# Window attention and a gated feed-forward on one core: neighbouring w_out rows, masks on TensorE, another order of loads

## Chip, core, metric

One core of one Trainium2 chip. The metric is the device time of one execution in microseconds; the number compared is the median of several executions. The engines are TensorE (PE, matmuls; its weight loads are PEld), VectorE (DVE), ScalarE (ACT), GpSimd (POOL) and SyncE (SP). Transfers are issued here from SyncE's queue and from GpSimd's, two from ScalarE's.

## What is computed

```python
# q, k, v: (4, 8, 768, 64) float32; n_sink = 4, window = 128
scores = (q @ k^T) / sqrt(64)
keep   = (key < 4) | ((0 <= query - key) & (query - key < 128))
a      = softmax(where(keep, scores, -1e9))
x      = (a @ v) with heads side by side          # (3072, 512)
h      = x @ w_in                                 # (3072, 2048)
g      = h * sigmoid(beta * h)                    # beta: one per column of h
out    = g @ w_out                                # (3072, 512) float32
```

The 2048 columns of h, the 2048 entries of beta and the 2048 rows of w_out belong together; any common order of them gives the same result.

## The kernel before

The 3072 tokens are eight blocks T of 384. A block's attention is four **units**, one for each pair of heads: units 0 to 3 make T=0, units 4 to 7 T=1, and so on to unit 31. Even blocks are the first half of a batch's sequence, odd ones the second half, whose queries also need the four sink keys.

A unit goes through these steps. q and k are loaded in float32 into a stage (`load_qk`, line 535, SyncE's queue), cast to bf16 on GpSimd or VectorE (`cast`, L650), transposed on TensorE into the PSUM bank "tr" (`transpose_in`, L663), and copied to SBUF (L670). TensorE makes the scores, ScalarE the exponential E, VectorE multiplies E by a 0/1 mask, TensorE multiplies E with v, the sink part first (L832), then the window (L843); a column of ones beside v gives the sums. VectorE takes their reciprocal (L852) and normalises (L854); the result is transposed (L871) and copied (L875) into xT, the input of the feed-forward. From unit 8 the last transpose, and from unit 12 the first one too, is done by the DMA; those later units have their q, k, v cast by the DMA on GpSimd's queue (`land_qk`, `land_v`).

Units 4 to 7 use `scores_by_banks`: the scores of a unit are split over two pairs of PSUM banks. Bank 0 has 512 columns for each head, bank 1 256 columns of window and 256 of sinks. Each bank has its own exponential (L795) and its own mask on VectorE (`mask_by_banks`, L804: 2x512 and 2x256 elements). Units 0 to 3 (`scores`, `PE_MASK` = 4) already mask on TensorE: a matmul of the identity with an additive mask (0 or -1e6) opens the accumulation, and the score matmuls add to it.

The feed-forward goes in **hidden blocks**: block i is the 128 columns m = i % 16 of h for the tokens of T = i // 16. Four matmuls of 384 columns (`hidden_matmul`, L887), a tanh on ScalarE (L895) and one operation on VectorE, the gate (L908), make g. Then **products** (`project`, L922) of 512 columns add g's part m times w_out's into an accumulator for each 128 tokens; after 16 of them the row block is copied and stored. Block T+1 of the hidden matmuls needs all four units of T+1.

w_in is loaded in four transfers, w_out in eight of two parts m each (`load_w_out`, L601, GpSimd's queue, cast to bf16 on the way). w_out's part m is the rows 128m to 128m+127, a row on each partition.

**The order on every engine is made by a planner** (class `Prog`): each operation has a guessed duration, and the planner simulates the engines and the queues and places at every step what can start first, the earlier in the program where two can. A DMA gets a landing time from sizes and rates (`transfer`), `TAIL` (900 ns) after its last byte, and some have an added lateness (`late`). The engines then execute that order strictly, waiting on semaphores wherever the guess was too early. Where the planner sees TensorE idle at the start, it inserts matmuls of ones (`filler`, L914), `MORE` (60 ns) beyond the hole it sees. The loads of SyncE's queue keep the program's order ("loads sp").

The part of the program that the change touches is written so:

```python
# steps s = -2 .. ; hidden block i = s for s < 16, then 8 steps without a block, then i = s - 8
casts = {-1: 4, 0: 5, 1: 6, 2: 7}          # casts of units 4 to 7
# units 4..7: transposes at s = 0..3, scores at s = 16..19, values at 17..20, out at 18..21
# products: none for s < 16, three a step in the 8 steps between, then two, then one a step
```

Of the kernel before, what the change touches and what calls it, by code (L numbers as in the profile page):

```python
# [11 lines left out]
DM, DF, NOUT = 512, 2048, 512  # L12
NTOK = B * S
# [5 lines left out]
TT = 384  # L19
# [27 lines left out]
PE_MASK = 4  # L47

# [49 lines left out]
class Prog:  # L98
# [14 lines left out]
    TAIL, MIX, HEAVY, RING = 900.0, 1.1, 2.5, 8  # L113
# [4 lines left out]
    IDLE, MORE, EARLY = 50.0, 60.0, 5500.0  # L118
# [251 lines left out]
def bass_streamingllm_window__then__act_swish_beta_kernel(  # L370
# [32 lines left out]
    beta_stage = sb("beta_stage", (16, 128), F32)  # L403
# [5 lines left out]
    ident32 = sb("ident32", (32, 32), F32)  # L409
    scratch = sb("scratch", (32, 1), F32)  # L410
    mask = [sb(f"mask{z}", (128, 6, 128), BF16) for z in range(2)]
    add_mask = sb("add_mask", (128, 6, 128), BF16)
    stage = {t: [sb(f"{t}_stage{z}", (128, 2, 6, D), F32) for z in range(4)] for t in "qk"}
# [116 lines left out]
    def load_qk(n, x, after=(), queue="sp"):  # L530
# [5 lines left out]
           dma=f"{name}{pb}_{half}", seq="loads " + queue, late=3300.0 if (n, x) == (4, 0) else 0.0,  # L536
# [55 lines left out]
    w_out_src = moe_w_out.rearrange("(m p) n -> p m n", p=128)  # L592
# [176 lines left out]
    def scores_by_banks(n):  # L769
# [3 lines left out]
        for bank, runs in enumerate(AT_ONCE[half]):  # L773
            of = 2 - 2 * bank
            names = HS_NAMES[of:of + 2]
            src = hs_ps[:, of:of + 2, :]
            with P.together("pe"):
# [7 lines left out]
                for kb, qb, nq in runs:  # L785
                    w = 128 * nq
                    for hh in range(2):
                        rows = slice(64 * hh, 64 * hh + 64)
                        op("pe", lambda e, at=at, w=w, kb=kb, qb=qb, nq=nq, hh=hh, rows=rows, of=of: e.matmul(  # L789
                            hs_ps[:, of + hh, at:at + w], keys_of(pb, rows, kb),  # L790
                            queries_of(pb, rows, qb, nq), start=True, stop=True),
# [7 lines left out]
    def mask_by_banks(n):  # L799
        z, half = n % NE, place(n)[2]  # L800
        for bank, cols in enumerate((slice(0, 512), slice(512, 768))):
            m = mask[half][:, :, :].rearrange("p m x -> p (m x)")[:, cols]
            w = cols.stop - cols.start
            op("dve", lambda e, m=m, cols=cols, w=w: e.tensor_tensor(  # L804
                E[z][:, :, cols], E[z][:, :, cols], m.unsqueeze(1).to_broadcast([128, 2, w]), ALU.mult),
               r=[("E", z, bank), *MASK[half]], w=[("E", z, bank)], **dve(580.0 if bank == 0 else 290.0))
# [77 lines left out]
    def hidden_matmul(i, c):  # L884
# [3 lines left out]
            bank, w_in16[:, c, m * 128:(m + 1) * 128], xT[:, c, T * TT:(T + 1) * TT],  # L888
# [31 lines left out]
    def project(T, t, m, bank, name, eng="act", cols=slice(0, NOUT), queue="sp"):  # L920
# [24 lines left out]
    op("act", lambda e: e.dma_start(beta_stage[:, :], moe_beta.rearrange("(m p) -> m p", p=128)),  # L945
       w=["beta_stage"], dma="beta", busy=500.0, lag=100.0)
# [6 lines left out]
    for c in range(3):  # L953
        load_v32(0, 1, c)
    op("act", lambda e: e.activation(scratch[:, :], ones32[:, 0:1], AF.Exp, bias=0.0, scale=1.0),
# [10 lines left out]
    select(ident32[:, :], ones32[:, :], [[1, 32]], ALU.is_equal, 0.0, 0, -1, ["ones32"], ["ident32"])  # L966
    transpose_first(0)
    op("pe", lambda e: nc.tensor.transpose(acc[1][:, 0:16], beta_stage[:, :], ident32[0:16, 0:16]),
       r=["beta_stage", "ident32"], w=["acc1"], **pe(64))
    op("dve", lambda e: e.tensor_scalar(beta_half[:, :], acc[1][:, 0:16], 0.5, None, ALU.mult),  # L970
       x=["acc1"], w=["beta"], **dve(100.0))
# [16 lines left out]
    for n in range(4):  # L988
# [4 lines left out]
        if n == 2:  # L993
# [4 lines left out]
            load_v32(1, 0, 0, [("w_in", 0, 4)])  # L998
            load_v32(1, 0, 1, [("w_in", 0, 4)])
            load_v32(1, 0, 2, [("w_in", 0, 4)])  # L1000
# [3 lines left out]
            load_qk(7, 1, [("w_in", 0, 4)])  # L1004
            load_v32(1, 1, 0, [("w_in", 0, 4)])
# [26 lines left out]
    for s in range(-2, S_END + NM):  # L1032
# [114 lines left out]
```

## Time and profile before

| | |
|---|---|
| three executions | 229.34, 230.49, 231.1 us; median 230.49 |
| the profiled execution | 229.0 us, of which the span of the instructions is 227.2 |
| granted TensorE clock | 1.00 throughout |
| busy: PE, DVE, ACT, POOL | 218.2, 133.0, 141.7, 125.4 us |
| weight loads PEld | 122.1 us, beside PE |
| moved by DMA | 29.7 MB in 98389 packets, 131 GB/s mean |
| first hidden block of T=0 / of T=1 | 17.07 us / 42.99 us from the span's start |

In a time order, a row gives start, length, engine, line, operation and tiles, how often, and in brackets how long the engine had been idle before and what ended that. The lengths shown for matmuls include their way through the array, so consecutive ones overlap; the distance between starts is what one costs in a run of them.

### The profile page before, as it was taken

To read this page: it belongs to the slowest core of one execution; us is meant where nothing else is said; L and a number is where in the kernel's file an instruction comes from. 1 tells how busy PE (TensorE), PEld (TensorE's weight loads), DVE (VectorE), ACT (ScalarE), POOL (GpSimd) and SP (SyncE) were. 2 spreads that over 40 slices of the span, in tenths; PEclk is the share of its full clock that TensorE was granted. 3 is DMA by queue.
4 is the path that set the end of the run, shared out by engine and by line. 5 is a ranking of instruction groups with operands and counts; after the bars stand their busy time and mean duration, and the time that the engine had idled before them with its cause. 6 is when DMAs were issued, how large, how long until landed. Compare 5 with 4: busy or idle time off the path is not lost.

```text
span 227.2 us, 4402 instructions
## 1 busy us (share of the span) xinstructions
PE 218.2 (96%) x1721; PEld 122.1 (54%) x1749; DVE 133.0 (59%) x263; ACT 141.7 (62%) x210; POOL 125.4 (55%) x193
## 2 busy tenths in 40 slices
PE   7999978899999999999999999999999999999995
PEld 4665545454655555555555555555555555555454
DVE  4756878459974666666565656555666564443200
ACT  3778796259855777666657676666656755555310
POOL 6692387999996969995939398876300000000000
PEclk9999999999999999999999999999999999999999
DMA  5999989999999989999979999999911112110122
GB/s 168 255 191 215 280 194 151 204 242 206 123 148 177 159 89 151 123 161 134 120 110 157 98 134 139 121 154 138 140 24 52 52 26 64 46 49 0 60 79 95
DMA packets 98389, 29.70 MB, mean 131 GB/s; under 512 B 84912, under 2 KB 95424, under 8 KB 98368
## 3 DMA queue, kind: packets, MB, share of 16 engines
q0 software_dynamic: 55888, 10.52, 58.2%
q1 hardware_dynamic: 42304, 18.75, 36.5%
q8 instruction: 14, 0.23, 0.4%
q10 hardware_dynamic: 176, 0.14, 0.2%
q14 instruction: 7, 0.06, 0.1%
HBM read 27.32 MB, written 6.29 MB: 148 GB/s over the span
## 4 chain that ended last, share of the span: by engine, by line
PE 73%; DMA 14%; SPq 6%; DVE 3%; issue 2%; POOL 1%; ACT 0%; ACTq 0%
PE hs_ps L887 31%; PE acc L922 30%; DMA k_stage<-in_k_dram 4%; PE hs_ps L754 4%; SPq L535 4%; PE hs_ps L843 3%; DMA q_stage<-in_q_dram 3%; DMA w_in<-in_moe_w_in_dram 3%; SPq L544 2%; DMA w_out<-in_moe_w_out_dram 2%; DMA xT<-o_norm 2%; PE hs_ps L922 2%; POOL qk L650 1%; PE hs_ps L832 1%; DVE g L908 1%
## 5 line engine op out<-in xcount | busy, mean ns | idle before, releaser
L895 ACT ACTIVATE th<-hs_ps,beta_half 128x384 f32<-128x384 f32 x120 | 69.3, 582 | 61.8 <-PE hs_ps L887 61.1
L887 PE MATMUL hs_ps<-xT,w_in 128*128 128x384 bf16 x480 | 96.2, 326 | 0.6 <-issue 0.2
L922 PE MATMUL acc<-w_out,g 128*128 128x512 bf16 x340 | 93.8, 380 | 1.3 <-issue 0.5
L908 DVE SCALAR_TENSOR_TENSOR g<-th,hs_ps 128x384 bf16<-128x384 f32 x120 | 65.5, 550 | 42.8 <-ACT th L895 41.3
L887 PEld LDWEIGHTS hs_ps<-xT,w_in 128*128 128x128 bf16 x480 | 45.6, 98 | 38.5 <-DVE g L908 1.2
L922 PEld LDWEIGHTS acc<-w_out,g 128*128 128x128 bf16 x368 | 33.6, 98 | 30.2 <-issue 3.8
L570 POOL DMA_DIRECT2D land<-in_q_dram x40 | 30.6, 767 | 15.9 <-DVE rden L852 15.9
L766 ACT ACTIVATE E<-hs_ps 128x1920 bf16<-128x1920 f32 (+1 forms) x20 | 32.8, 1640 | 0.3
L811 DVE TENSOR_TENSOR E<-E,mask 128x1536 bf16<-128x1536 bf16 x20 | 19.2, 959 | 21.2 <-ACT E L766 21.2
L570 POOL DMA_DIRECT2D land<-in_k_dram x40 | 30.6, 767 | 0.0
L579 POOL DMA_DIRECT2D v_aug<-in_v_dram x40 | 30.6, 767 | 0.0
L930 ACT ACTIVATE out_sb<-acc 128x512 f32<-128x512 f32 x23 | 13.7, 597 | 7.3 <-PE acc L922 7.1
L843 PE MATMUL hs_ps<-v_aug,E 128*128 128x65 bf16 x348 | 17.3, 193 | 0.1
L843 PEld LDWEIGHTS hs_ps<-v_aug,E 128*128 128x128 bf16 x348 | 15.7, 97 | 2.7 <-issue 1.3
L854 DVE TENSOR_TENSOR o_norm<-hs_ps,rden 128x384 bf16<-128x384 f32 x29 | 16.1, 556 | 1.0
L727 ACT ACTIVATE E<-hs_ps 128x768 bf16<-128x768 f32 x16 | 12.6, 814 | 1.9 <-PE hs_ps L720 1.7
L832 PE MATMUL hs_ps<-v_sink,E 128*128 128x130 bf16 x48 | 9.3, 219 | 1.1 <-DVE E L804 1.1
L754 PE MATMUL hs_ps<-qkT 64*128 64x256 bf16 (+2 forms) x144 | 10.1, 254 | 0.0
L795 ACT ACTIVATE E<-hs_ps 128x1024 bf16<-128x1024 f32 x8 | 7.8, 1038 | 2.2 <-PE hs_ps L789 2.2
L650 POOL CAST qk<-k_stage 128x384 bf16<-128x384 f32 x12 | 6.3, 526 | 4.8 <-DMA k_stage<-in_k_dram 4.5
L852 DVE RECIPROCAL rden<-hs_ps 128x6 f32<-128x6 f32 x29 | 5.6, 193 | 3.8 <-PE hs_ps L843 3.7
L914 PE MATMUL acc<-ones 128*128 128x384 bf16 (+1 forms) x32 | 6.7, 344 | 1.2 <-DVE ones L457 1.2
(73 smaller groups left out, 148.1 us busy)
## 6 DMA issues: line engine op xcount, KB each, us to landing
out_dram<-out_sb SPq DMA_DIRECT2D x23, 256.0 KB, 2.7
q_stage<-in_q_dram SPq DMA_DIRECT2D x12, 192.0 KB, 6.4
k_stage<-in_k_dram SPq DMA_DIRECT2D x12, 192.0 KB, 6.2
w_in<-in_moe_w_in_dram POOLq DMA_DIRECT2D x4, 512.0 KB, 6.5
w_out<-in_moe_w_out_dram POOLq DMA_DIRECT2D x8, 256.0 KB, 5.9
land<-in_q_dram POOLq DMA_DIRECT2D x40, 48.0 KB, 3.7
land<-in_k_dram POOLq DMA_DIRECT2D x40, 48.0 KB, 3.6
v_aug<-in_v_dram POOLq DMA_DIRECT2D x40, 48.0 KB, 3.5
```

What stands on the lines that cost most here:

```text
L570: op("gp", lambda e, d=d, s=s: e.dma_start(d, s), w=[("land", pb, half, x, hh)], after=after, dma=f"l{pb}{half}{x}{hh}", **transfer(TT * D ...
L579: op("gp", lambda e, d=d, s=s: e.dma_start(d, s), w=[("v", pb, 3 * half + c, hh) for c in range(3)], after=after, dma=f"lv{pb}{half}{hh}", ...
L754: op("pe", lambda e, at=at, w=w, kb=kb, qb=qb, nq=nq, hh=hh, rows=rows, bank=bank: e.matmul(hs_ps[:, of + 2 * hh + bank, at:at + w], keys_ ...
L766: op("act", lambda e: e.activation(dst, src, AF.Exp, bias=0.0, scale=SCALE), x=list(names), w=[("E", z, 0), ("E", z, 1)], **act(1920 if ha ...
L811: op("dve", lambda e: e.tensor_tensor(E[z][:, :, 0:768], E[z][:, :, 0:768], m.unsqueeze(1).to_broadcast([128, 2, 768]), ALU.mult), r=[("E" ...
L843: last=(x == len(kbs) - 1): e.matmul(av_ps[:, at + hh * D1:at + hh * D1 + D1], E[z][:, hh, col:col + 128], v_aug[:, pb, hh, kb, 0:D1], sta ...
L854: op("dve", lambda e: e.tensor_tensor(o_norm[o][:, :, :, :].rearrange("p m h d -> p (m h) d"), src[:, :, 0:D], rden[z][:, :].unsqueeze(2). ...
L887: op("pe", lambda e: e.matmul(bank, w_in16[:, c, m * 128:(m + 1) * 128], xT[:, c, T * TT:(T + 1) * TT], start=(c == 0), stop=(c == 3)), r= ...
L895: op("act", lambda e: e.activation(th[i % 3][:, :], bank, AF.Tanh, bias=0.0, scale=beta_half[:, m:m + 1]), x=[name], r=["beta"], w=[("th", ...
L908: op("dve", lambda e: e.scalar_tensor_tensor(g[T % 2][:, m, :], th[i % 3][:, :], 1.0, bank, ALU.add, ALU.mult), r=[("th", i % 3)], x=[name ...
L922: op("pe", lambda e: e.matmul(bank[:, 0:width], g[T % 2][:, m, t * 128:(t + 1) * 128], w_out16[:, m, cols], start=(m == 0), stop=(m == NM ...
L930: op("act", lambda e: e.activation(out_sb[z][:, 0:width], bank[:, 0:width], AF.Copy, bias=0.0, scale=0.5), x=[name], w=[("out_sb", z)], ** ...
```

## The change

- **w_out's rows.** With `PER = 4`, part m = 4g + j now holds the rows 512g + 4p + j on partition p. Four parts of one g are then neighbouring rows of w_out on each partition, and a transfer of 4 (or 2) parts reads 8 KB (4 KB) in one piece there. There are five transfers (2, 2, 4, 4, 4 parts). The weights of the hidden matmuls become every fourth column of w_in16, and beta is read in the same order: its load moves from ScalarE's queue, with a transpose on TensorE, to SyncE's queue in pieces of four numbers, straight to its place.
- **Masks.** For bank 0 of units 5, 6 and 7 TensorE opens the accumulation with the identity times an additive mask (`add_mask1`, made from `mask[1]` by one GpSimd operation); their VectorE masks on bank 0 go. Unit 4 and all masks of bank 1 stay.
- **Copies.** The copies L670 of units 5 and 7 go from ScalarE to VectorE.
- **Loads.** On SyncE's queue q, k of units 6 and 7 come ahead of v of T=1. The transfers of w_out wait for other loads.
- **The planner's numbers.** `TAIL` 1100 for 900, `MORE` 0 for 60, 2300 ns of lateness for q of unit 8, other rates for w_out and other durations for the masks L804. With them the order on all engines is another.

```diff
+PER = 4
+PE_MASK_BANKS = ((5, 0), (6, 0), (7, 0))
-    TAIL, MIX, HEAVY, RING = 900.0, 1.1, 2.5, 8
+    TAIL, MIX, HEAVY, RING = 1100.0, 1.1, 2.5, 8
-    IDLE, MORE, EARLY = 50.0, 60.0, 5500.0
+    IDLE, MORE, EARLY = 50.0, 0.0, 5500.0
...
-           ... late=3300.0 if (n, x) == (4, 0) else 0.0,
+           ... late=3300.0 if (n, x) == (4, 0) else 2300.0 if (n, x) == (8, 0) else 0.0,
...
-    w_out_src = moe_w_out.rearrange("(m p) n -> p m n", p=128)
+    w_out_src = moe_w_out.rearrange("(g p j) n -> p g j n", p=128, j=PER)
...
-        op("gp", lambda e: e.dma_start(w_out16[:, m:m + ms, :], w_out_src[:, m:m + ms, :]), after=after,
+        op("gp", lambda e: e.dma_start(w_out16[:, m:m + ms, :].rearrange("p j n -> p (j n)"),
+                                         w_out_src[:, m // PER, m % PER:m % PER + ms, :].rearrange("p j n -> p (j n)")), after=after,
-           dma=f"wo{m}", **transfer(ms * 128 * NOUT * 4, 350, 740.0, 3.0))
+           dma=f"wo{m}", **transfer(ms * 128 * NOUT * 4, 410 if ms == 4 else 385, 740.0, 3.0))
... scores_by_banks
+            masked = (n, bank) in PE_MASK_BANKS
+            if masked:
+                cols = slice(0, 512) if bank == 0 else slice(512, 768)
+                with P.together("pe"):
+                    for x in range(2):
+                        op("pe", lambda e, x=x, of=of, cols=cols: e.matmul(
+                            hs_ps[:, of + x, 0:cols.stop - cols.start], ident[:, :], add_mask1[:, cols],
+                            start=True, stop=False, skip_group_check=True),
+                           r=["ident", "add_mask1"], w=[names[x]], **pe(cols.stop - cols.start))
-                            queries_of(pb, rows, qb, nq), start=True, stop=True),
+                            queries_of(pb, rows, qb, nq), start=not masked, stop=True,
+                            skip_group_check=masked),
... mask_by_banks
+            if (n, bank) in PE_MASK_BANKS:
+                continue
... hidden_matmul
-            bank, w_in16[:, c, m * 128:(m + 1) * 128], xT[:, c, T * TT:(T + 1) * TT],
+            bank, w_in16[:, c, m // PER * 512 + m % PER:m // PER * 512 + 512:PER], xT[:, c, T * TT:(T + 1) * TT],
... the program
-    op("act", lambda e: e.dma_start(beta_stage[:, :], moe_beta.rearrange("(m p) -> m p", p=128)),
-       w=["beta_stage"], dma="beta", busy=500.0, lag=100.0)
+    op("sp", lambda e: e.dma_start(beta_raw[:, :].rearrange("p (g j) -> p g j", j=PER),
+                                   moe_beta.rearrange("(g p j) -> p g j", p=128, j=PER)),
+       w=["beta_raw"], dma="beta", seq="loads sp", busy=500.0, lag=300.0)
...
             load_qk(5, 1, [("w_in", 0, 4)])
-            load_v32(1, 0, 0, [("w_in", 0, 4)])        # and (1, 0, 1), (1, 0, 2): now after unit 7's
             load_qk(6, 0, [("w_in", 0, 4)])
...
+    op("gp", lambda e: e.tensor_scalar(
+        add_mask1[:, :], mask[1][:, :, :].rearrange("p m x -> p (m x)"), -1.0, -NEG, ALU.add, ALU.mult),
+       r=MASK[1], w=["add_mask1"], busy=1000.0, lag=140.0, after=[("v", 3, 0, 0)])
...
-                transpose_in(n, eng="act" if n in (5, 7) else "dve")
+                transpose_in(n, eng="act" if n in () else "dve")
...
-            load_w_out(2, 2, [("k_stage", 2, 1)])
-            load_w_out(4, 2, [("k_stage", 2, 1)])
-            load_w_out(6, 2, [("k_stage", 3, 1)])
+            load_w_out(2, 2, [("v_stage", 0, 0)])
+            load_w_out(4, 4, [("k_stage", 3, 1)])
...
-            load_w_out(8, 2, [("v_stage", 1, 2)])      # and (10, 2), (12, 2), (14, 2)
+            load_w_out(8, 4, [("v_stage", 1, 2)])
+            load_w_out(12, 4, [("v_stage", 1, 2)])
```

More of the change, by code (lines that the diff above doesn't have):

```diff
@@ L535, in load_qk @@
         op(queue, lambda e: e.dma_start(d, s), w=[(name + "_stage", pb, half)], after=after,
-           dma=f"{name}{pb}_{half}", seq="loads " + queue, late=3300.0 if (n, x) == (4, 0) else 0.0,
+           dma=f"{name}{pb}_{half}", seq="loads " + queue, late=3300.0 if (n, x) == (4, 0) else 2300.0 if (n, x) == (8, 0) else 0.0,
            **transfer(2 * TT * D * 4, 290 if n > 3 else 180 if n == 1 else 330, 520.0, 5.0 if 4 <= n < 8 else 1.0))
@@ L805, in mask_by_banks @@
                 E[z][:, :, cols], E[z][:, :, cols], m.unsqueeze(1).to_broadcast([128, 2, w]), ALU.mult),
-               r=[("E", z, bank), *MASK[half]], w=[("E", z, bank)], **dve(580.0 if bank == 0 else 290.0))
+               r=[("E", z, bank), *MASK[half]], w=[("E", z, bank)], **dve(700.0 if bank == 0 else 330.0))
     def mask_at_once(n):
```

21 lines of the change are left out of this document (8 added, 13 removed).

## Prediction

> **What bounds the kernel now.** I read the page first (busy shares, slices, chain), then the time order of TensorE, VectorE, GpSimd and SyncE over the first 60 us, then the groups kept apart by shape.
>
> ```profile
> PE 218.2 (96%) x1721; PEld 122.1 (54%) x1749; DVE 133.0 (59%) x263; ACT 141.7 (62%) x210; POOL 125.4 (55%) x193
> PE   7999978899999999999999999999999999999995
> PE 73%; DMA 14%; SPq 6%; DVE 3%; issue 2%; POOL 1%; ACT 0%; ACTq 0%
> ```
>
> The reader is to see that TensorE (PE) is the bound, that the only weak slices after the start are 28 to 45 us, and that the chain outside PE is loads. So the whole bill is PE work plus the holes in PE. PE's shown lengths overlap; I count by pitch, from the chain: four 384-column matmuls of L887 in 0.65 us are 162 ns each, three 512-column ones of L922 in 0.65 us are 216 ns each.
>
> The holes lie where the first token block (T=0) has no hidden blocks left and the second (T=1) cannot start before units 4 to 7 are through attention. That stretch, by windows (columns: length, then busy time of PE, PEld, DVE, ACT, POOL):
>
> ```profile
> 28.50:43.00 14.50, 12.56 (x149) 7.15 (x151) 11.06 (x24) 9.69 (x12) 12.18 (x20) 1.00 1.00 175
> 43.00:50.00 7.00, 6.18 (x38) 3.00 (x37) 3.03 (x6) 2.52 (x5) 6.35 (x10) 1.00 1.33 241
> ```
>
> 12.56 us looks full, but by pitch the work of the first row is: 29 transposes at 0.055 = 1.6, four units' half-array scores (768 columns, the two heads side by side) 4 x 0.32 = 1.3, 8 sink scores at 0.109 = 0.9, attention values 12 x 0.056 + 48 x 0.03 = 2.1, 17 products (L922) at 0.216 = 3.7, in all 9.6. So 4.9 of the 14.5 us are holes. About 2.0 of these I take as changes between full- and half-array matmuls, two into and two out of it per unit (the list of waits shows 20 such for L754 with 4.4 us of "issue" on the weight load; 16 at 0.12 is 2.0); some 2.9 us are waits. What ends them is seen on PE and on VectorE (DVE):
>
> ```profile
> 33.26 0.23 PE L832 MATMUL hs_ps<-v_sink,E 128*128 128x130 bf16 x1 [0.76 <-DVE E L804]
> 35.82 0.23 PE L832 MATMUL hs_ps<-v_sink,E 128*128 128x130 bf16 x1 [0.32 <-DVE E L804]
> 45.48 0.34 PE L663 MATMUL hs_ps<-ident,qk 128*128 128x128 bf16 x3 [0.82 <-POOL qk L650]
> ```
> ```profile
> 30.96 2.24 DVE L804 TENSOR_TENSOR E<-E,mask 128x1024 bf16<-128x1024 bf16 x2 [1.06 <-ACT E L795]
> 33.13 0.94 DVE L670 COPY qkT<-hs_ps 128x768 bf16<-128x768 bf16 x1
> 34.00 0.68 DVE L804 TENSOR_TENSOR E<-E,mask 128x1024 bf16<-128x1024 bf16 x1
> 38.43 0.69 DVE L804 TENSOR_TENSOR E<-E,mask 128x1024 bf16<-128x1024 bf16 x1 [0.47 <-ACT E L795]
> 42.98 0.36 DVE L875 COPY xT<-hs_ps 128x384 bf16<-128x384 bf16 x1 [0.44 <-PE hs_ps L871]
> ```
>
> From 30.96 to 43.34 DVE does nearly nothing but the masks, copies and normalisations of units 4 to 7, one behind the other; unit 6's queries and keys wait in PSUM until 33.13 behind unit 4's masks. PE's values (L832) wait for the masks.
>
> **The change, part by part.**
>
> *TensorE masks bank 0 of units 5 to 7.* Six added matmuls of 512 columns: 6 x 0.216 = **+1.3 us of PE work**. Three DVE masks of 128x1024 go: in their rows 0.68 to 0.69 each, 2.1 us in all. The added matmuls need only the identity and the new mask, and a free bank; the cover is ScalarE's exponential of the other bank (L795, 1.04 us), against 2 x 0.216 of mask and about 0.2 of scores. Without the cover they stand at their full 1.3 us.
>
> *Copies of units 5 and 7 from ScalarE to DVE.* ScalarE's were 0.79 each, DVE's 0.95. DVE gets 1.9 us back, ScalarE loses 1.6 of its 9.69. So DVE's sum hardly moves; what moves is when: the copies can go under the last gates of T=0 (the last L908 starts 29.35), the masks stood after them.
>
> *q, k of units 6, 7 ahead of v.* GpSimd's casts show the old order: units 4, 5 from 24.00, v at 28.89, unit 6 at 30.21, unit 7 at 31.96. Twelve loads of one queue keep their sum, so units 6 and 7 come some 2 us earlier and the first v some 2 us later, at about 31. The values of unit 4 began at 33.26, so v is late by nothing as long as it is cast by 33. Each moved load takes SyncE's queue 0.47 to 2.5 us, whichever stands first; the sum stays.
>
> Together: DVE's run from 30.96 loses three masks (2.1) and unit 6's copy (0.94, now before it) and gains at worst unit 7's copy (0.95). I let the first T=1 block start 2.1 us earlier, at about 40.9; bounds 0 and 3.0. In PE's bill: holes 4.9 down to 2.4 (the waits almost gone, the 2.0 of changes staying), so -2.5, and +1.3 of work: **-1.2 us**. Bounds: +1.3 if no wait goes, -1.6 if all 2.9 go.
>
> *Loads that the planner reckons later* (2300 ns on unit 8's q, the tail 1100 for 900). In the third PE line above PE stood 0.82 us, at a time when other T=1 blocks were ready, because the transposes of unit 8 were ordered for a load that came at 44.9. Ordered later, T=1 work fills that: **-0.8**; bounds -1.0 (the hole by pitch) and 0.
>
> *w_out in runs of 2 or 4 rows.* Eight transfers become five: three issues at 0.716 less on GpSimd, in the stretch where it is 12.18 of 14.5 busy. Each partition now reads 4 or 8 KB in one piece instead of 2 KB. No row shows this; bounds: no gain, or the best packet of 8192 bytes among the trace's packet records (307 ns, 26.7 B/ns, against w_in's and w_out's 2048 read in 98 ns, 20.9), which takes a fifth off the 3.1 MB read in fours, some 2 us of landing. I take half. Products resume at 37.44 and unit 8's q is asked for at 37.38, both behind w_out; PE can do other work then, so on the path I put **-0.2**; bounds -0.6 and +0.3 (w_out 4 and 5 now land only with 6 and 7).
>
> *Strided weights.* L887 now loads every fourth column (8 bytes apart). Its weight load is 98 ns under a matmul of 162. Bounds from strided rows: ScalarE's strided copy 485 ns against 479 straight (L688, L875), DVE's 539 against 352. 98 x 1.53 is 150, still under 162: **0**, with the matmul as cover; from 1.65 times on it costs.
>
> *Start.* PE's transpose of beta (L968, 0.28), a GpSimd select (0.2) and the 60 ns of extra filler on each of eight groups go; beta comes behind v on SyncE's queue in 512 pieces of 16 bytes, before q, k of unit 4. Its price has no row: 0, or 512 pieces over 16 engines at the mean packet of that queue, 31 ns (36.5% of 16 x 227.2 us by 42304 packets), 1.0 us on the w_in that gates unit 4. The mask's preparation on GpSimd (about 0.84 us, from 0.29 for 128 and 0.51 for 384 columns) falls where GpSimd then idles 5.17 us before 24.00. I take **-0.2**; bounds -0.5 and +0.6.
>
> After 50 us PE's work is the same; the order changes, and I give it nothing.
>
> Sum: -1.2 -0.8 -0.2 +0 -0.2 = **-2.4 us**, on the profiled execution's 229.0 (span 227.2 and 1.8 around it) 226.6. The median shown, 230.49, stands 1.5 over that execution; the same step from it gives **228.1**.
>
> **Rivals.**
>
> *The masks eat the gain.* If DVE, with its copies, sets T=1's start as before (its sum changes by 0.2 us only), the holes are filled by the 1.3 us of added work and nothing else falls: -0.8 and twice -0.2 remain, 229.3. For it: DVE's unchanged sum. Against it: unit 6's copy stood behind masks by 2 us.
>
> *Slower: v starves behind w_out.* The trace shows what a stream of weights on GpSimd's queue does to SyncE's: q of unit 4 was issued at 17.84 and cast only at 24.00, while 2.7 us is the quickest such landing. The 4-row w_out waits only for unit 7's k, which now lands before v. Then up to 1.6 MB read (4.7 us at the 334 GB/s of 16 x 20.9) go ahead of v of units 6, 7, which land near 38 instead of 33; their values, at 38.25 and 41.01 before, end 0.5 to 3 later than before (the shift of 5 less the 2 that the units gain, or part of it), the masks add 1.3, unit 8's 0.8 stays a gain: +1.0 to +3.5, so 232.7. It decides from the point where v of units 6, 7 is cast after 37. Against it: GpSimd must cast unit 7 and start the transfer first, by when half of v has passed. The Trainium skill (DMA: Bandwidth & Descriptors, "Queues, rings and completion order") has each engine take turns between queues by whole packets; larger w_out packets would then take a larger share. That speaks for this rival.
>
> *Strided weights cost.* Twice 98 is 196, 34 over the pitch, times 512 loads: +17 us, 245. No strided row is that bad. The Trainium skill (Advanced Engine Details and Errata, "SBUF Cachelines") names a penalty where accesses change the 16-byte line and asks for at least two on each; four bf16 apart gives exactly two, the edge of it, so by that rule this rival does not come, and it would at twice the step. No run here shows that edge.
>
> *The new order gives more.* If it also takes the 0.4 us of other holes before 50 and half of the 1.7 that I count from 50 to 60: another -1.3, 226.8.
>
> **How the numbers follow.** Forecast 0.50 (226.3 to 229.5), masks eat the gain 0.22, more gain 0.10, v starves 0.12, strided weights 0.06. A measurement of this kernel tells about 1%, 2.3 us. Faster by over 1% (under 228.2): two thirds of the forecast, most of it lying just under the line, plus nearly all of the larger gain, and a little of the first rival: 0.45. Slower (over 232.8): the strided weights, half of v's case, some of the unknown orders, 0.16. Within: 0.39. The range leaves out strided weights and the ends: 226.0 to 232.3.
>
> **What would show it.** Right: L804 with five instructions, unit 6 and 7's casts before v's, the first T=1 block of L887 at 40 to 41.5 instead of 42.99, no wait of L663 on POOL near 45, L887's weight load near 98 ns, five w_out issues. Wrong: that block at 42.5 or later; v cast after 37 with L843 waiting for POOL; PEld of L887 over 150 ns; holes past 50 us that were not there.

## The result, and the profile after

The changed kernel is **slower**, by about 1%: 234.56 us as the median of 20 executions (230.57 to 237.72), against 229.93 for the kernel before (228.23 to 234.22, 20 executions). The ratio is **1.0107 [1.0077, 1.0137]**, some 2.5 us, where 228.1 was forecast. Of the 20 executions 12 ran at a mean granted clock of 0.985 to 0.993, with a median of 236.4; the ratio leaves the long ones out, and the profile below is of an execution at 1.0: 231.5 us, span 229.8 (before 229.0 and 227.2). Lines below are those of the changed kernel: L903 hidden blocks (before L887), L938 products (L922), L786 the new mask matmuls, L820 VectorE masks (L804), L848/L859 attention values (L832/L843), L654 casts (L650), L552 v casts (L549), L604 w_out (L601).

From the page: busy sums, TensorE's slices, and the chain that ended last.

```profile
PE 220.6 (96%) x1755; PEld 129.7 (56%) x1755; DVE 131.8 (57%) x262; ACT 141.1 (61%) x208; POOL 122.6 (53%) x190
PE   7899999899997999799999999999999999999995
PE 73%; DMA 11%; POOL 6%; issue 4%; DVE 2%; SPq 1%; ACT 1%; POOLq 0%; ACTq 0%
```

Of the weak slices at 28 to 45 us one 8 is left. Two new ones stand further on, the thirteenth (69 to 75 us) and the seventeenth (92 to 98). In the chain's line shares "DMA xT<-o_norm 4%" is the third entry.

The two windows that answer to those of the prediction (length, then busy time of PE, PEld, DVE, ACT, POOL):

```profile
28.90:44.50 15.60, 14.91 (x164) 8.33 (x163) 10.59 (x24) 8.72 (x10) 9.97 (x18) 1.00 1.01 181
44.50:50.00 5.50, 5.50 (x35) 3.08 (x33) 2.68 (x5) 3.05 (x6) 5.18 (x9) 1.00 1.42 243
```

TensorE is busy for 14.91 of 15.60 us and then for all of 5.50; the 0.82 us wait for unit 8 is not there. By pitch the holes from 28.5 to 50 us fell from 6.2 to 3.15. But the first T=1 block stands at 44.48, later than the 42.99 of before: the holes were filled with products (24 ahead of that block, 20 before the change) and with the masks, not by an earlier T=1.

TensorE in time order at the three places where it now waits for a transfer:

```profile
42.58 1.04 PE L938 MATMUL acc<-w_out,g 128*128 128x512 bf16 x4 [0.62 <-DMA w_out<-in_moe_w_out_dram]
...
69.50 0.65 PE L903 MATMUL hs_ps<-xT,w_in 128*128 128x384 bf16 x3
71.64 1.00 PE L903 MATMUL hs_ps<-xT,w_in 128*128 128x384 bf16 x5 [1.49 <-DMA xT<-o_norm]
72.48 0.22 PE L848 MATMUL hs_ps<-v_sink,E 128*128 128x130 bf16 x1
...
93.77 0.65 PE L903 MATMUL hs_ps<-xT,w_in 128*128 128x384 bf16 x3
95.58 0.35 PE L903 MATMUL hs_ps<-xT,w_in 128*128 128x384 bf16 x1 [1.17 <-DMA xT<-o_norm]
```

The first T=2 block begins at 69.50, does the three matmuls for which xT is there, and stands until the fourth piece has come through the DMA transpose; the first T=3 block does the same. By pitch the two holes are 1.65 and 1.33 us. Before the change unit 12's values stood ahead of that block, and its eight matmuls came with a hole of only 0.25 us:

```profile
69.84 0.22 PE L832 MATMUL hs_ps<-v_sink,E 128*128 128x130 bf16 x1
...
70.39 1.72 PE L887 MATMUL hs_ps<-xT,w_in 128*128 128x384 bf16 x8
```

In the changed kernel these values are queued behind the block (72.48). The chain that ended last has the transfer itself, from the end of the normalisation to the landing, first before and then after the change:

```profile
66.78 4.30 DMA xT<-o_norm
```
```profile
66.35 5.24 DMA xT<-o_norm
90.78 4.76 DMA xT<-o_norm
```

From T=4 on (119.81, before 117.14, with 138 products planned ahead of it in both) the two executions keep a constant distance of 2.6 to 2.7 us: after 120 us nothing is gained or lost.

VectorE and GpSimd in the same stretch:

```profile
31.27 1.02 DVE L820 TENSOR_TENSOR E<-E,mask 128x1024 bf16<-128x1024 bf16 x2
32.21 0.95 DVE L674 COPY qkT<-hs_ps 128x768 bf16<-128x768 bf16 x1
...
39.24 0.36 DVE L891 COPY xT<-hs_ps 128x384 bf16<-128x384 bf16 x1 [1.37 <-PE hs_ps L887]
...
43.82 0.36 DVE L891 COPY xT<-hs_ps 128x384 bf16<-128x384 bf16 x1 [1.25 <-PE hs_ps L887]
```
```profile
25.86 0.50 POOL L654 CAST qk<-q_stage 128x384 bf16<-128x384 f32 x1 [6.41 <-DMA q_stage<-in_q_dram]
27.02 0.51 POOL L654 CAST qk<-k_stage 128x384 bf16<-128x384 f32 x1 [0.66 <-DMA k_stage<-in_k_dram]
...
32.21 0.96 POOL L552 CAST v_aug<-v_stage 128x384 bf16<-128x384 f32 x2
34.11 0.96 POOL L552 CAST v_aug<-v_stage 128x384 bf16<-128x384 f32 x2 [0.94 <-DMA v_stage<-in_v_dram]
```

VectorE's closed run of masks is broken up and now waits for TensorE. Unit 4's q and k were cast at 25.86 and 27.02 (before 24.00 and 25.78), and T=0's last hidden block, between the transposes that wait for them, slipped from 28.31 to 28.90. In this execution v did not starve: the second pair was cast at 34.11.

### The profile page after: what moved, and what is told of

It is laid out like the page before. It is cut to its first block, busy times and chain, and to the rows that moved or that the text cites. A ratio compares the mean times of both kernels' runs of the same rounds, so it can differ in the third digit from the quotient of the medians.

```text
span 229.8 us, 4434 instructions
## 1 busy us (share of the span) xinstructions
PE 220.6 (96%) x1755; PEld 129.7 (56%) x1755; DVE 131.8 (57%) x262; ACT 141.1 (61%) x208; POOL 122.6 (53%) x190
## 4 chain that ended last, share of the span: by engine, by line
PE 73%; DMA 11%; POOL 6%; issue 4%; DVE 2%; SPq 1%; ACT 1%; POOLq 0%; ACTq 0%
PE acc L938 32%; PE hs_ps L903 30%; DMA xT<-o_norm 4%; PE hs_ps L859 4%; PE hs_ps L758 3%; DMA w_out<-in_moe_w_out_dram 3%; DMA k_stage<-in_k_dram 2%; DMA v_stage<-in_v_dram 2%; POOL qk L654 2%; PE hs_ps L938 2%; POOL v_aug L552 1%; POOL w_in L599 1%; SPq L538 1%; PE hs_ps L848 1%; PE hs_ps L747 1%
## 5 line engine op out<-in xcount | busy, mean ns | idle before, releaser
L938 PE MATMUL acc<-w_out,g 128*128 128x512 bf16 x368 | 100.2, 380 | 0.6 <-DMA w_out<-in_moe_w_out_dram 0.6
L903 PE MATMUL hs_ps<-xT,w_in 128*128 128x384 bf16 x480 | 96.6, 327 | 2.8 <-DMA xT<-o_norm 2.7
L903 PEld LDWEIGHTS hs_ps<-xT,w_in 128*128 128x128 bf16 x480 | 53.1, 114 | 36.4 <-DMA xT<-o_norm 3.4
L938 PEld LDWEIGHTS acc<-w_out,g 128*128 128x128 bf16 x368 | 33.7, 98 | 29.7 <-issue 3.2
L859 PE MATMUL hs_ps<-v_aug,E 128*128 128x65 bf16 x348 | 17.3, 193 | 0.0
L859 PEld LDWEIGHTS hs_ps<-v_aug,E 128*128 128x128 bf16 x348 | 15.8, 97 | 2.2 <-issue 1.1
L848 PE MATMUL hs_ps<-v_sink,E 128*128 128x130 bf16 x48 | 9.3, 219 | 0.0
L674 DVE COPY qkT<-hs_ps 128x768 bf16<-128x768 bf16 x8 | 7.6, 952 | 1.2 <-PE hs_ps L667 1.2
L654 POOL CAST qk<-k_stage 128x384 bf16<-128x384 f32 x12 | 6.1, 510 | 4.0 <-DMA k_stage<-in_k_dram 3.6
```

Source lines behind the costliest of these rows:

```text
L859: last=(x == len(kbs) - 1): e.matmul(av_ps[:, at + hh * D1:at + hh * D1 + D1], E[z][:, hh, col:col + 128], v_aug[:, pb, hh, kb, 0:D1], sta ...
L903: op("pe", lambda e: e.matmul(bank, w_in16[:, c, m // PER * 512 + m % PER:m // PER * 512 + 512:PER], xT[:, c, T * TT:(T + 1) * TT], start= ...
L938: op("pe", lambda e: e.matmul(bank[:, 0:width], g[T % 2][:, m, t * 128:(t + 1) * 128], w_out16[:, m, cols], start=(m == 0), stop=(m == NM ...
```

## The experiments

Labels e1 to e18 are in the order of running. Each ratio is to the kernel before on the same chip; the chips differ (before 229.4 on one, 231.6 on another), so only ratios are compared across chips. Even so the change itself, repeated as e10, came out at 1.0031 for 1.0107: a difference of under 0.8% shows nothing by itself unless the two ran together on one chip, as e1 to e4 did, e5 to e8, e9 to e11, e12 to e15 and e16 to e18.

**The first T=2 block, reckoned later (e1).**

```diff
-               r=[("o_norm", z)], w=[("xT", T, hp)], dma=f"x{z}", busy=1190.0, lag=650.0)
+               r=[("o_norm", z)], w=[("xT", T, hp)], dma=f"x{z}", busy=1190.0, lag=1300.0)
```

> The changed kernel, with one guess of the planner raised: the DMA transposes into xT are reckoned at 1300 ns instead of 650. TensorE's order stays the same up to T=2's first block, which now stands behind unit 12's values and some products. Theory 'order': the two waits for xT at the starts of T=2 and T=3 (1.49 us and about 1.2 us in the list, 3.0 us of holes by pitch) are there only because a block stands in front of work that is ready; then both go, the span falls from 229.8 to 227.0-227.8, ratio to the kernel before 0.998-1.003. Rival 'chain': the attention of units 8 to 15 is itself too late; TensorE runs out of other work and the holes reappear before or behind the block; span 229 or more, ratio 1.007-1.011.

The profiled execution took 228.13 us with a span of 226.4, 3.4 below the change's. Here its first T=2 block, on TensorE:

```profile
71.24 1.46 PE L903 MATMUL hs_ps<-xT,w_in 128*128 128x384 bf16 x8
```

Eight matmuls, no wait. The ratio is nevertheless 1.0132 [1.0073, 1.0192]: it rests on other executions, of 230.65 to 234.76 us, which were not traced. What the trace settles is the rival that the hole only moves elsewhere: T=4 begins at 116.46, before 119.81 in the change and 117.14 ahead of it. For the time, e9, e11 and e15 had to be run.

**The masks' width (e2).**

```diff
-  hs_ps[:, of + x, 0:cols.stop - cols.start], ident[:, :], add_mask1[:, cols],
+  hs_ps[:, of + x, 0:128], ident[:, :], add_mask1[:, 0:128],
```

> The changed kernel with the six added mask matmuls 128 columns wide instead of 512, all guesses and the order unchanged (so three quarters of the bank-0 masks of units 5 to 7 are left out). It takes 6 x (216 - 56) = 0.96 us of TensorE work out. Theory 'masks are paid': that work lies on the path, span 228.8-229.1, ratio 1.006-1.008. Rival 'masks are hidden': T=2's start waits for xT of unit 11 anyway, whose chain does not run through the masks; the wait at 71.6 grows by what the masks save, span 229.5-229.8, ratio 1.009-1.011.

Three quarters of the added masks are left out here. 1.0069 [1.0029, 1.0109], 0.4% under the change, with overlapping intervals: of the size of the work taken away (six times 512 columns to 128), and no proof. Its trace showed something else, on VectorE:

```profile
14.95 0.48 DVE L972 TENSOR_SCALAR beta_half<-beta_raw 128x16 f32<-128x16 f32 x1 [2.31 <-DMA beta_raw<-in_moe_beta_dram]
15.03 0.40 DVE L868 RECIPROCAL rden<-acc 128x6 f32<-128x6 f32 x1
```

VectorE stands 2.31 us for beta, with unit 1's normalisation right behind. The change's own profile has this operation at 12.60 with no such wait.

**w_out in twos (e3), masks back on VectorE (e4), fours behind v (e5).**

```diff
 # e3; the other two fours likewise
-            load_w_out(4, 4, [("k_stage", 3, 1)])
+            load_w_out(4, 2, [("k_stage", 3, 1)])
+            load_w_out(6, 2, [("k_stage", 3, 1)])
 # e4
-PE_MASK_BANKS = ((5, 0), (6, 0), (7, 0))
+PE_MASK_BANKS = ()
 # e5
-            load_w_out(4, 4, [("k_stage", 3, 1)])
+            load_w_out(4, 4, [("v_stage", 1, 2)])
```

> The changed kernel with w_out's last twelve parts in six transfers of two parts (4 KB a partition in one piece) instead of three of four, with the same loads awaited before them. Theory 'fours land late': TensorE's wait of 0.62 us for w_out at 42.58 goes, unit 8's q is asked for after two parts instead of four and its cast comes before 46.2 (44.9 before the change), units 8 to 11 come 0.5-1 us earlier, T=1's first block at 43.6-44.0 instead of 44.48; ratio 1.003-1.007. Rival 'size of the transfer does not matter': same landings, ratio 1.009-1.012. The planner places anew, which alone may move the time by some 0.5 us.

> The changed kernel without masks on TensorE: units 5 to 7 have their bank-0 masks on VectorE again, all else as changed. Theory 'masks are paid': TensorE loses 1.3 us of work, VectorE gets 2.1 us back in the stretch before T=1; if TensorE's work is what counts the ratio falls to 1.004-1.006. Rival 'masks are hidden, VectorE sets T=1': T=1's first block moves from 44.48 to 45 or later and the ratio is 1.011 or more.

> The changed kernel with one trigger moved: the first w_out transfer of four parts waits for the last v of T=1 instead of unit 7's k. In the run without masks on TensorE the profile caught v behind that transfer: v of units 6, 7 cast at 38.85 after 4.15 us of waiting, then TensorE waiting 4.69 us for the w_out queued behind that cast. Theory 'v starves behind the fours': this is what lengthens many executions of the changed kernel (230.6 to 237.7); with the trigger moved no execution has it, all lie within 2.5 us of each other and below 233.5, the granted clock is 0.999 or 1.000 in all. Rival 'it is not the order of these two': the spread stays, some executions at 234 to 238. The shortest execution need not be shorter, since w_out comes later: 229.5 to 231.5.

e3: 1.0103 [1.0069, 1.0137]. e4: 1.0173 [1.0120, 1.0226]. e5: 1.0093 [1.0051, 1.0135]. None undoes the loss, and all three traces have the wait for beta (2.2, 2.6 and 2.6 us). e4's profiled execution (span 234.8) is the first in which v starves: the second pair of v casts at 38.85, after 4.15 us of waiting, and products waiting 4.69 us for w_out at 47.47. With a first T=1 block at 51.17 it says nothing on the masks; e13 had to. In e5, where the fours wait for v, v is cast by 35.56 and the twelve executions lie between 231.18 and 234.53, where the change's reach 237.72; two of them are still past the 233.5 that was expected as the end.

**The rows alone (e6), everything but the rows (e7).** e6 is the kernel before with the rows, the strided weights and beta's new load; e7 has the rest of the change, with w_out in the old layout and twos.

```diff
 # e6: before, with
+PER = 4
+    w_out_src = moe_w_out.rearrange("(g p j) n -> p g j n", p=128, j=PER)
...
 # e7: after, without these
```

> The kernel before with the dealt rows alone: PER = 4, strided weights, beta by SyncE's queue; w_out in eight transfers of two parts as before, masks, copies, loads and the planner's numbers as before. Theory 'rows cost little': weight load of the hidden matmuls 114 ns instead of 98 under a matmul of 162, first T=0 block within 0.3 us, ratio 0.998-1.004. Rival 'rows carry the loss': unit 4's q is late (25.9 instead of 24.0 in the changed kernel) through beta's small pieces and w_out's longer packets, T=1's first block 43.5 or later, ratio 1.006-1.012.

> The other half: the kernel before with the masks on TensorE, the copies on VectorE, q, k of units 6, 7 ahead of v, the planner's numbers; rows, beta and w_out's rows as before, w_out in transfers of two parts with the changed triggers. Theory 'rows carry the loss': ratio 0.995-1.002. Rival 'masks and order carry it': 1.3 us of mask work and a first block of T=2 or T=3 that waits for xT, ratio 1.006-1.012. No execution should have v behind a transfer of four.

e6: **1.0114 [1.0049, 1.0180]**; e7: **1.0006 [0.9966, 1.0047]**. By this pair the rows looked like the loss; e15 to e18 did not bear that out. In e6's trace unit 8's q, behind w_out, is cast at 48.66 (before 44.92):

```profile
49.22 0.50 PE L665 MATMUL hs_ps<-ident,qk 128*128 128x128 bf16 x3 [3.75 <-POOL qk L652]
```

e7's trace shows why the other half brought nothing:

```profile
72.69 0.65 PE L901 MATMUL hs_ps<-xT,w_in 128*128 128x384 bf16 x3
74.90 0.99 PE L901 MATMUL hs_ps<-xT,w_in 128*128 128x384 bf16 x5 [1.55 <-DMA xT<-o_norm]
```

The hole before T=2 is there without any rows. It comes from the new order.

**The step of the weights (e8).** T=2, 3 read w_in16 in steps of 8 columns, T=4, 5 of 16, T=6 of 2, T=7 of 1.

> The changed kernel with other steps between the weight columns of the hidden matmuls by block: 4 for T=0, 1 as changed, 8 for T=2, 3, 16 for T=4, 5, 2 for T=6, 1 for T=7 (so the columns of w_in in T=2 to 7 are not those that w_out's rows belong to). The order is the same. If two accesses per 16-byte line are what counts, the weight load is 98 at steps 1 and 2, 114 at 4 as measured, and clearly more at 8 and 16 (150 to 250); if the load only grows with the step, 130 at 8 and 160 at 16; over 162 the matmuls of L903's successor line come apart and T=4 to 5 gets longer by 64 x 2 times the excess.

TensorE's weight loads of L907 in windows of T=0 (step 4), T=2 (8), T=4 (16) and T=6 (2); after "|" the busy time and the mean ns of one:

```profile
L907 PEld LDWEIGHTS hs_ps<-xT,w_in 128*128 128x128 bf16 x32 | 3.5, 113 | 1.4
L907 PEld LDWEIGHTS hs_ps<-xT,w_in 128*128 128x128 bf16 x52 | 7.1, 145 | 2.6 <-DMA xT<-o_norm 1.4 <-issue 0.2
L907 PEld LDWEIGHTS hs_ps<-xT,w_in 128*128 128x128 bf16 x53 | 7.7, 144 | 2.6
L907 PEld LDWEIGHTS hs_ps<-xT,w_in 128*128 128x128 bf16 x53 | 5.2, 98 | 4.4
```

98 ns at 2 columns, 113 at 4, 145 at 8, 144 at 16: a strided load costs up to half as much again and then no more. The matmul's pitch is 162, so all of it stays hidden.

**beta's operation behind T=0's last xT (e9), and the pieces of w_out (e10).**

```diff
 # e9
+    op("dve", lambda e: e.tensor_scalar(beta_half[:, :], beta_raw[:, :], 0.5, None, ALU.mult),
+       r=["beta_raw"], w=["beta"], after=[("xT", 0, 3)], **dve(100.0))
 # e10
-  w_out16[:, m:m + ms, :].rearrange("p j n -> p (j n)")      # and the same of the source
+  w_out16[:, m:m + ms, :]
```

> The changed kernel with one VectorE operation moved: beta's halving, which VectorE takes up in its strict order before unit 1's normalisation and which in the profiles of five variants waits 2.2 to 3.0 us for beta's 16-byte pieces, now stands behind the last copy of T=0's attention. TensorE's order is the same. Theory 'beta blocks VectorE': that wait goes, T=0's first block comes at 17.0-17.4 (18.2 to 20.7 in those profiles), executions lose their upper part: fast ones 229.5-231, ratio 1.001-1.006. Rival 'beta is not needed to explain it': T=0 at 18.5 or later in the profile, or tanh waits for beta instead, ratio 1.009-1.012.

> The changed kernel with the same five transfers of w_out, same rows, same order on all engines, but each partition's 8 or 4 KB given as four or two pieces of 2 KB, so that the packets are those of the kernel before. Theory 'long packets starve SyncE's queue': v of units 6, 7 no longer waits about 4 us and unit 8's q comes before 45.5; no execution over 234, clock 0.993 or more in all, median 231-232 instead of 234.6. Rival 'the transfer's size and early start do it, not its packets': the same spread to 236-238, median 233.5 or more. The fast ones keep beta's wait and the xT waits: ratio 1.006-1.011.

e9: 1.0046 [0.9996, 1.0096]; the wait for beta is gone and T=0 begins at 16.71 (17.17), the xT waits stay (a hole of 1.26 at T=2). e10's edit did nothing: neighbouring pieces were joined again, and 384 packets of 4096 bytes were written as in the change. It is a repeat of the change (1.0031 [0.9988, 1.0073]; over all its executions the median is 236.44 for 231.60), and its profiled execution, span 238.5, shows GpSimd waiting longest for v:

```profile
40.39 0.96 POOL L552 CAST v_aug<-v_stage 128x384 bf16<-128x384 f32 x2 [6.41 <-DMA v_stage<-in_v_dram]
41.30 1.05 POOL L604 DMA_DIRECT2D w_out<-in_moe_w_out_dram  x2
```

**The edits of e1, e9 and e10 together (e11).**

> The changed kernel with three things mended together: pieces of 2 KB in w_out's transfers, beta's halving behind T=0's attention, the transposes into xT reckoned at 1300 ns. If the loss is beta's wait (about 1.5 us), long packets and the xT waits (up to 3 us) beside the mask work of 1.3 us that stays, then the span is 226.0-227.5, the ratio 0.988-0.998, no execution over 231. If the masks' work or the order of loads carried it, the ratio stays at 1.004 or more.

**0.9942 [0.9907, 0.9977]**: with beta's operation moved and xT reckoned later (the third edit is void) the changed kernel beats the one before. In its trace neither block waits (T=2 at 77.05 and T=3 at 98.81, eight matmuls each without a break). Against e9, run together with it on one chip, the number for xT and the order that follows from it are the only difference: 1.0%, 2.4 us, and the intervals lie apart.

**With w_out in twos as well (e12), then without the masks (e13), and with v first again (e14).**

```diff
 # e12 is e11 with e3's twos; e13 is e12 with e4's line; e14 is e12 with
+            load_v32(1, 0, 0, [("w_in", 0, 4)])   # and (1, 0, 1), (1, 0, 2)
             load_qk(6, 0, [("w_in", 0, 4)])
```

> The changed kernel with three things undone: w_out's 4-row loads are 2-row loads at the same places, the operation that halves beta stands behind T=0's last xT copy on VectorE, and the planner reckons a DMA-transposed xT with 1300 ns for 650. Theory (the loss is w_out's large transfers ahead of v, the beta wait, and first blocks of T=2 and T=3 ordered ahead of ready work; the masks, copies and load order bring what was forecast): ratio 0.985 to 0.992, span 223.5 to 225.5, v of units 6, 7 cast before 36 with a wait below 2 us in POOL's list, no wait of PE on xT or w_out over 0.5 us at T=2 and T=3. Rival (the three are small and the masks or the load order carry the loss): ratio 1.000 to 1.008.

> The kernel of the run before without the TensorE masks: VectorE masks all scores of units 5 to 7 again. Theory (masks cost TensorE 1.3 us and take 2.1 us from VectorE's run ahead of T=1, so they are worth up to 1 us): 0.5 to 1 us longer than the run before, the first T=1 block 1 to 2 us later. Rival (mask work is paid for in full, because VectorE's run no longer sets T=1): 0.8 to 1.3 us shorter than the run before.

> The kernel with the three undone, but v of units 4 to 7 asked for ahead of q, k of units 6 and 7 again, as before the change. Theory (the load order is part of what closes the holes between 28 and 43 us): 0.5 to 1.5 us longer than with q, k first. Rival (the order of these loads is worth nothing once w_out leaves SyncE's queue its share): within 0.4 us of it.

e12: 1.0052 [1.0019, 1.0086]. My theory of that moment, that w_out's fours make the loss and twos mend it, **fell**: 0.985 to 0.992 was expected. e13: 1.0048 [1.0013, 1.0082], and e14: 1.0019 [0.9980, 1.0057]: within the intervals neither the masks nor the load order are worth anything either way. e12's profiled execution began late, on GpSimd's queue:

```profile
20.67 0.57 POOL L604 DMA_DIRECT2D w_out<-in_moe_w_out_dram  x1 [2.34 <-DMA w_in<-in_moe_w_in_dram]
```

w_in's second transfer landed at 20.38, 1.8 us later than in the change's own (18.60), and unit 4's k was cast at 29.20.

**The order without the rows (e15).** e7 with e1's edit.

> The kernel before with everything of the change but the rows of w_out and beta's load, and the planner's 1300 ns for xT. Theory (without the rows, what was forecast is there in full once xT is reckoned late enough: minus 1.2 and minus 0.8): ratio 0.988 to 0.993, no PE wait on xT over 0.5 us near 70 to 75. Rival (the hole at 73 us only moves to other work): ratio 0.998 to 1.002.

**0.9951 [0.9921, 0.9982]**, 228.70 us against 230.03 on that chip, all 12 executions between 227.68 and 229.84; a smaller gain than the 0.988 to 0.993 that was expected. The first T=2 block:

```profile
72.28 1.51 PE L901 MATMUL hs_ps<-xT,w_in 128*128 128x384 bf16 x8
```

e7 differs from it by that one number, 650 against 1300: 0.55% or 1.3 us for the waits on xT, with intervals that overlap by 0.16% and on another chip, so the surer figure is that of e9 and e11.

**beta's load alone (e16), the rows in twos (e17) and in fours (e18),** each on top of e15. In e17 and e18 beta comes as it did before the change, without SyncE's load and VectorE's wait for it.

```diff
 # e16: e15 with a load that nobody reads
+    op("sp", lambda e: e.dma_start(beta_raw[:, :].rearrange("p (g j) -> p g j", j=4),
+                                   moe_beta.rearrange("(g p j) -> p g j", p=128, j=4)), ...
 # e17: e15 with PER = 4 and w_out in twos; e18: the same with 2, 2, 4, 4, 4
```

> The kernel of e15 (order without rows, ratio 0.9951) with one load added: beta's 512 pieces of 16 bytes behind v on SyncE's queue, into a tile that nothing reads; beta itself comes as before. If the pieces hold up SyncE's queue and the first w_in, the ratio is 1.000 to 1.006, with unit 4's q cast 0.5 to 1.5 us later. If beta's part is only VectorE's wait for it, nothing changes: 0.993 to 0.997.

> The kernel of e15 with the rows of w_out dealt in neighbours and loaded two at a time (2048 bytes written in a piece for 1024), and the strided weights; beta comes as before, so it is paired with other rows than it belongs to (the only part of the computation that differs). If the larger pieces take SyncE's share, the ratio is 1.002 to 1.006 and the first T=1 block stands at 46 to 47.5 for 44.5. If beta's load was the cost, 0.993 to 0.997 and 44 to 45.

> The same with w_out in the changed kernel's two 2-row and three 4-row loads; beta paired with other rows again. If the size of the pieces sets the loss, it is at least that of the run before, with some executions 3 us longer (v waiting 3 us and more). If fours in themselves were the better form, as the 0.9942 of e11 beside the 1.0052 of e12 has it, the ratio is 0.990 to 0.996.

e16: 0.9953 [0.9915, 0.9990]; the load itself is free. e17: 0.9985 [0.9944, 1.0025]. e18: 0.9930 [0.9886, 0.9974]; over all its executions the median is 232.14 for 231.60, and the profiled one (span 231.6) has v starving, on GpSimd and then on TensorE:

```profile
38.59 0.96 POOL L553 CAST v_aug<-v_stage 128x384 bf16<-128x384 f32 x2 [5.20 <-DMA v_stage<-in_v_dram]
```
```profile
45.58 1.10 PE L939 MATMUL acc<-w_out,g 128*128 128x512 bf16 x4 [3.14 <-DMA w_out<-in_moe_w_out_dram]
```

The packet records of these two traces tell how. In e18 SyncE's 256-byte packets of v carry 260 KB between 30 and 32 us; once w_out's 4096-byte packets run, 46 KB (32 to 34) and 57 KB (34 to 36), with v still coming until 38. In e15, with packets of 1024 bytes, the same queue moves 152 KB between 32 and 34 and v is done. In packets the two shares are of one order: 224 of SyncE's to 98 of GpSimd's in e18 (34 to 36), 613 to 193 in e15 (32 to 34). In bytes they are not: 57 KB to 328, and 152 to 195. So the larger packet takes the bytes. The Trainium skill (DMA: Bandwidth & Descriptors, "Queues, rings and completion order") has each engine go round its queues packet by packet; the traces agree that it is not by bytes, at about 1 to 2.3 and 1 to 3.2; an even 1 to 1 they do not show, and no run shows whether the skill's packets are the records counted here.

## Why the prediction was wrong

The step that failed is "After 50 us ... the order changes, and I give it nothing": the new order costs 3.0 us there, in two waits for xT. Two accounts show it, one by the trace and one by the time.

By the trace, up to T=4's first block at equal products: the holes from 28.5 to 50 us minus 2.4, the masks plus 1.3, T=0's end plus 0.6, the two waits for xT plus 3.0. The sum is plus 2.5; the traces stand 2.67 apart. Against the forecast of minus 2.4 that is 4.9 us: 3.0 from xT, 0.9 from holes that were sized too large, 0.8 from the start and 0.2 from w_out.

By time, on one chip and run together: the change's repeat 1.0031 (e10), with beta's operation moved 1.0046 (e9), with xT reckoned later as well 0.9942 (e11). The number for xT is worth 2.4 us; that moving beta's operation gains time is not shown. What is left in e11, without the waits, is a gain of 1.3 us over the kernel before, of the 2.4 forecast.

- **Holes of the first stretch, "4.9 down to 2.4" and unit 8's wait, minus 0.8 (together minus 3.3).** The mechanism came as told: window 44.50 to 50.00 is full and L667 no longer waits. The size was off. Corrected it is minus 2.4: the trace of before lacks the records of 28 of 400 products, three of them before 50 us (30 weight loads, 27 matmuls), and each missing record reads as a hole of 0.22, so 6.2 is really some 5.5, and the forecast's 4.9 some 4.2; a new wait of 0.62 for w_out takes a part back. "The first T=1 block start 2.1 us earlier" failed: 44.48. The sign named for that, 42.5 or later, was there, and in this the rival "the masks eat the gain" was nearer.
- **Masks, plus 1.3, against three VectorE masks.** Paid as forecast (six matmuls of L786), with VectorE's run broken up, and in the end worth nothing: e13 against e12 is minus 0.04%. The load order is worth nothing either (e14 against e12, minus 0.3%, inside the intervals). So the minus 1.2 that I booked for these parts was not found; unit 8 and the planner's numbers are what the minus 1.1 us of e15 can still come from. That share was not tried by itself.
- **"After 50 us ... the order changes, and I give it nothing." This step failed most.** The term was put at nothing without a reason. The planner reckoned 650 ns after its 1190 for the DMA transpose; the chain has 5.24 and 4.76 us from o_norm to xT. The new order puts the first T=2 block 0.9 us earlier (69.50 for 70.39), ahead of unit 12's values, while the last piece of its xT lands 0.5 us later (66.35 plus 5.24, before 66.78 plus 4.30). Plus 3.0 us in the trace; 2.4 us in time (e9 to e11, intervals apart) and 1.3 (e7 to e15, intervals that overlap). Holes past 50 us were among the forecast's own signs of being wrong.
- **Start, minus 0.2.** The price I asked of beta's load was the wrong one. Its 512 packets took 9 ns each, not 31, and e16 finds it free. What waits is VectorE's operation, queued in order ahead of unit 1's normalisation, when the load lands late: 1.7 to 3.0 us in six traces (e2 to e5, e8, e10), nothing in the change's and 0.3 in e1's. In those six T=0 begins at 18.2 to 20.7 for 17.17, but the ratios do not show what that costs (e9 beside e10). I did not ask what stands behind the waiting instruction. In the change's own profile the plus 0.6 comes from unit 4's q and k, cast 1.9 and 1.2 us later than before.
- **w_out's rows, minus 0.2.** The best packet that the forecast went by is one of queue "q14 instruction" and no load of this kind; w_out's packets came near it, the landing did not follow. In the stretch from 24 to 62 us the median packet of 8192 bytes read (4096 written) took 324 ns, of 4096 read 173, and of 2048 read, before the change, 98: 25, 24 and 21 bytes per ns. With the slow packets the means are 389, 185 and 107 ns: 21, 22 and 19. Yet the median landing of a w_out transfer rose from 5.9 to 7.2 us; it is 7.1 in e15, which has the old rows, so the rise is there without the new rows. The ratios of e15, e17 and e18 (0.9951, 0.9985, 0.9930) show neither gain nor loss from the rows themselves; over all executions fours are longer, 232.14 (e18) beside 230.50 on the same chip without the rows (e16).
- **Strided weights, 0.** Right: 114 ns in the changed kernel, under 162, though above the "near 98" that I named as the sign. The Trainium skill's rule of two hits on a 16-byte line (Advanced Engine Details and Errata, "SBUF Cachelines") promised full speed at this step; measured, the load already takes 15 ns more than 98 there, and 47 more at the next (e8).
- **The rival "v starves behind w_out", 0.12.** It exists, with the place and the sign that I gave: v cast at 37.8 to 40.4, past the 37 named as its point, and T=1 begun at 48.4 to 53.0 for 44.5 (e4, e8, e10, e11, e18). The price is above the 1.0 to 3.5 us that I gave where it can be read: the traced execution of e11 took 233.97 us, 4.1 over the median of its eleven. It is not what the ratio of 1.0107 measures: in the change's own profile v is cast at 34.11. But e10 is the same kernel as the change, and its traced execution, of 240.36 us, has v starving; how often the change does that was not traced, and 0.12 may have been too little. "GpSimd must cast unit 7 and start the transfer first" is a race, and which way it goes differs from execution to execution.

What stays open: e12 (1.0052, twos) beside e11 (0.9942, fours) and e17 (0.9985, twos). That twos are the worse form is not shown, since e12's profiled execution starts late with w_in, and it ran on another chip. Open too is why the rows alone cost 1.1% in the old order (e6) and nothing clear of the intervals on top of e15; e6's traced execution shows the wait of 3.75 us for unit 8's q. Whether v starves was traced in single executions only.

## What to carry to other kernels

An order that a planner writes is only as good as the latency it reckons with: a change that closes holes early moves later work forward into waits that the old order had covered, so look up the first consumer of each long transfer and compare the reckoned with the traced time. For each load that is moved ask which operation takes it up and what stands behind that operation on its engine; the load itself may be free. Before a hole in a trace is priced, count the records: products that are missing look like idle time.

## What the runs showed of the hardware

- Weight loads of 128 columns took 98 ns with columns 1 or 2 apart, 113 at 4, 145 at 8 and 144 at 16 (bf16, e8).
- Beside packets of 4096 bytes written, the other queue's traffic fell from 260 to 46 KB in 2 us (e18, 30 to 32 and 32 to 34 us); beside those of 1024 it kept 152 (e15, 32 to 34).
- Pieces that are neighbours on both sides were joined into one packet, so writing them apart in the access pattern changed nothing (384 packets of 4096 bytes in e10 and in the change).
- Where TensorE stood for 3 us and more, the execution's mean granted clock was 0.985 to 0.993 (e4, e6, e10, e11, e18); in the change's profile, with its longest hole at 1.65 us, it was 1.0. The mean comes from one piece at half the clock: 0.5 for 3.4 us in e11 (from 47.9, the hole ended at 46.97) and e18, for 6.8 us in e4, e6 and e10 (in e10 from 47.2, within the hole that ended at 49.27). 3.4 us at half the clock are 1.7 us lost to TensorE where it has work, on top of the hole.
- Shorter holes went both ways: e9 and e14 (0.992 and 0.993) had such a piece of 3.4 us right at the end of holes of 1.6 and 1.5 us, e2, e7 and e12 had holes of 1.7, 1.6 and 1.7 us and none near them, so the length of one hole is not the whole rule.
